# A decode-attention kernel: TensorE's unrolled matmuls put into loops, two weights loaded ahead of a third, and the output's heads split otherwise

## The chip, the cores and the metric

The kernel runs on one NeuronCore of a Trainium2 chip. Its engines are TensorE (PE: matmuls, with a weight load of its own, PEld), VectorE (DVE), ScalarE (ACT), GpSimd (POOL) and SyncE (SP, which issues DMAs); each runs its own program and they meet at semaphores. Sixteen DMA engines move data between HBM and the on-chip memory. The metric is the device time of one execution in microseconds; lower is better.

## The reference

One step of decoding for a batch of 2, one new token each, D = 512. Both halves start from `xn = layernorm(x)`.

```python
q = xn @ wq                       # 32 query heads of 128, from 512 x 4096 weights
scores = q . k * 128**-0.5        # 8 kv heads, 4 query heads share one; 32768 keys each
s = (softmax(scores) . v) @ wo    # 4096 x 512 weights

h  = gelu(layernorm(xn) @ w1); ... @ w2      # S = 1: every shifted part of it is padding
x1 = xn + 0
g  = silu(x1 + gelu(layernorm(x1) @ w3) @ w4)   # F = 1792
out = x + s * g
```

With one token the shifts of the w1/w2 branch push every row out, so its contribution is zero, and the kernel loads neither weight. The caches, 2 x 8 x 32768 x 128 in bf16 each for k and v, are nearly all of the data.

## The kernel before, in words

A *group* is one (batch, kv head) pair; there are 16. For each, 8 MB of K and 8 MB of V are loaded, each by one DMA from SyncE's queue (the last group's in halves). K has three slots of 4 MB in `kbuf`, V two in `vbuf`: K of group m+1 takes the one free slot and the one whose scores are finished first, V of group m+1 the place of V of group m.

**SyncE's queue** fixes the order of the loads: wq, w3, w4 and K of group 0 without a wait (L310 to L313), two small ones for x, V of group 0 once the w4 matmuls are done (L454; w3 and w4 lie in `vbuf`), four small ones for g (L457), then K and V of groups 1 to 15 by turns (L461 to L473), and last the output weights wo in six parts (L474 to L479). K of group m waits for TensorE's last use of the slot's old scores (`pe.sem`, raised at L703), V of group m for ScalarE's count of finished groups (`ac.sem`, L495).

**The prologue** (L333 to L459) makes xn, its second layernorm, constants out of an identity, and from 4 small transposes the columns `xT`. Then come 32 matmuls with wq (L403, four column strips of TensorE side by side) into `sc[0]` and `sc[1]`, two VectorE transposes (L408), q_sb, one spreading matmul (L413), and `qr` (L416). GpSimd makes from it, for every group, the weights `z` of the score matmuls (L505, L506). After that stand 16 matmuls with w3 (L424), the gelu on VectorE and ScalarE, 14 matmuls with w4 (L439), and silu, which gives g.

**A group.** VectorE transposes K in 16 pieces (L589) through four buffers `T`. TensorE makes the scores in two halves, `sc[0]` and `sc[1]`, of 8 x 4 matmuls each (L698). Between the halves stand 4 f32 matmuls that gather the *previous* group's output, `oT` (`head_oT`, L660), and in the second half, after its fifth piece, one that turns it, `xp` (`head_xp`, L666). VectorE takes the maxima (`peak`, L568), scales the previous group's output (`head_on`, L543 to L552), and picks its row (`head_out`, L559 to L565). A matmul of `S` (L710) spreads the maxima, ScalarE takes the exponential (L491), VectorE transposes it (L608), and TensorE multiplies with V (L722, 2 x 32 matmuls), with small filler matmuls ahead (`fill`, L673); a last matmul sums the exponentials (L729). TensorE counts the turn in a register and branches back (L733, L734).

**The output** (L737 to L774) gathers the last group, then applies wo. Heads 0 to 3 use one wide matmul (L740) that spreads their outputs, VectorE's `own_part` (L630, L634), and 16 matmuls into `qrb`. Head k = 4, below `KC` = 5, adds 4 matmuls of 512 columns there (L760). For heads 5 to 7, 4 x 4 matmuls of 128 columns each go straight into `pro` (L768). ScalarE copies `qrb` to `wsum` (L646), and 4 f32 matmuls with `comb` (L750, eight passes) add that to `pro`, ahead of head 6's. VectorE multiplies with g and adds x (L647, L648), and two DMAs store it.

`LateQueue` keeps the prologue's TensorE instructions and `place()` writes them out just ahead of the loop. `take(eng, s, n)` waits for a semaphore and lowers it by what it waited for. `t_tv` counts TensorE's steps for VectorE (`used`, `sum_of`, `out_of`, `turned` give the counts), `t_vt` VectorE's steps for TensorE.

Of the kernel before, what the change touches and what calls it, by code (L numbers as in the profile page):

```python
# [7 lines left out]
F32 = mybir.dt.float32  # L8
# [13 lines left out]
T_BUFS = 4  # L22
# [44 lines left out]
class LateQueue(Queue):  # L67
# [13 lines left out]

    def place(self):
        for emit, need, inc in self.kept:
            for s, v in need[:-1]:
# [34 lines left out]
def kernel(  # L119
# [37 lines left out]
    KC = 5  # L157
# [19 lines left out]
    Ts = [sb(f"T{i}", [128, W], I32) for i in range(T_BUFS)]  # L177
# [38 lines left out]
    qT = Ts[0].bitcast(F32)  # L216
# [13 lines left out]
    sc = [bank(f"sc{i}") for i in range(NPART)]  # L230
# [49 lines left out]
    t_vt, t_vg, t_tv = (sem(f"t_{n}") for n in ("vt", "vg", "tv"))  # L280
# [7 lines left out]
    wq3 = kbuf_wq[:, 0:DK * HD].rearrange("p (k f) -> p k f", k=DK)  # L288
    W4O = DK * Fdim
# [17 lines left out]
    with tc.tile_critical(sync_engine=mybir.EngineType.Pool, no_gpsimd_drain=True):  # L307
        nc.scalar.wait_ge(t_shift, n_out).then_inc(t_shift, -n_out)

        sp.op(lambda e: e.dma_start(out=kbuf_wq[:, 0:DK * HD], in_=A_wq.rearrange("(p k) f -> p (k f)", k=DK)), inc=(d_wq, 16))  # L310
# [17 lines left out]
        po.op(lambda e: e.memset(ob[:, :], 0.0), inc=(t_ob, 1))  # L328
# [5 lines left out]
        ve.op(lambda e: e.memset(S[:, 0:NPART * rep], 1.0), inc=(t_tv, 1))  # L334
        ve.op(lambda e: e.memset(pro[:, :], 0.0))
        ve.op(lambda e: e.memset(sc[0][:, :], 0.0))
        e_s00 = ve.op(lambda e: e.memset(sc[1][:, :], 0.0))
        e = ve.op(lambda e: e.tensor_copy(out=xf[:, :], in_=x_bf[:, :]), (d_x, 16))
# [51 lines left out]

        treg = qrb[:, :].bitcast(BF16)
        for k in range(DK):
# [4 lines left out]
            in_=treg[:, 0:64 * DK].rearrange("p (k s c) -> p s k c", k=DK, s=2)[:, :, :, 0:B]), e, (d_wq, 16))  # L397
        HH = Hq // NPART
        for i in range(NPART):
            for k in range(DK):  # L400
                for n in range(NQ):
                    last = k == DK - 1 and n == NQ - 1
                    e = pe.op(lambda t, i=i, k=k, n=n: t.matmul(  # L403
                        sc[i][32 * n:32 * n + B, :], lhsT=xT[:, k, :],
                        rhs=wq3[:, k, :].rearrange("p (h n y) -> p h n y", n=NQ, y=32)[:, i * HH:(i + 1) * HH, n, :],
                        start=(k == 0), stop=(k == DK - 1), tile_position=(0, 32 * n)),
                        e_xT, e_s00, inc=last)
            e = ve.op(lambda v, i=i: v.transpose(out=qT[:, i * 512:(i + 1) * 512], in_=sc[i][:, :]), e)  # L408
# [9 lines left out]


        FQ = Fdim // NQ  # L420
        for k in range(DK):
            for n in range(NQ):
                last = k == DK - 1 and n == NQ - 1
                e = pe.op(lambda t, k=k, n=n: t.matmul(  # L424
                    pro[32 * n:32 * n + B, 0:FQ], lhsT=xT[:, DK + k, :],
                    rhs=w3v[:, k, n * FQ:(n + 1) * FQ].rearrange("p (y f) -> p f y", y=32),
                    start=(k == 0), stop=(k == DK - 1), tile_position=(0, 32 * n)), (d_w3, 16), inc=last)
        e = ve.op(lambda v: v.transpose(out=h4[:, :], in_=pro[:, 0:FQ]), e)
        e_hf = ve.op(lambda v: v.tensor_copy(
            out=hf[:, :].rearrange("p (f b) -> p f b", b=B), in_=h4[:, :].rearrange("p (f c) -> p f c", c=32)[:, :, 0:B]), e)  # L430
        e = ve.op(lambda v: v.tensor_mul(out=x2[:, :], in0=hf[:, :], in1=hf[:, :]), e_hf)
        e = ve.op(lambda v: v.tensor_scalar(out=x2[:, :], in0=x2[:, :], scalar1=0.044715, scalar2=1.0, op0=ALU.mult, op1=ALU.add), e)
        e = ve.op(lambda v: v.tensor_mul(out=inner[:, :], in0=hf[:, :], in1=x2[:, :]), e)
        e = ac.op(lambda v: v.activation(out=th[:, :], in_=inner[:, :], func=ACT.Tanh, scale=GELU_C), e)
        e = ve.op(lambda v: v.tensor_scalar(out=th[:, :], in0=th[:, :], scalar1=0.5, scalar2=0.5, op0=ALU.mult, op1=ALU.add), e)
        e = ve.op(lambda v: v.tensor_mul(out=h_bf[:, :], in0=hf[:, :], in1=th[:, :]), e, (d_w4, 16))
        h2 = sc[1]
        for f in range(FK):
            e_h2 = pe.op(lambda t, f=f: t.matmul(  # L439
                h2[0:B, :], lhsT=h_bf[:, f * B:(f + 1) * B], rhs=w4v[:, f, :],  # L440
                start=(f == 0), stop=(f == FK - 1)), e, inc=f == FK - 1)
        e_tf = ve.op(lambda v: v.tensor_add(out=t_f[:, :], in0=xn[:, :], in1=h2[0:B, :]), e_h2)
        e = ac.op(lambda v: v.activation(out=sig[:, :], in_=t_f[:, :], func=ACT.Sigmoid), e_tf)
        e_g = ve.op(lambda v: v.tensor_mul(out=g[:, :], in0=t_f[:, :], in1=sig[:, :]), e)
# [16 lines left out]
        for m in range(1, NG):  # L461
            base = m % 2
            if m < NG - 1:
                sp.op(lambda e, m=m, base=base: e.dma_start(
                    out=kbuf[:, base * SLOT:(base + NPART) * SLOT], in_=row_view(A_k_cache, *groups[m])),
                    (pe.sem, pe_0 + m), e_q, inc=(t_k[0], 16))
            else:
                for i, h in enumerate(order(m)):
                    sp.op(lambda e, m=m, h=h, base=base: e.dma_start(
                        out=kbuf[:, (base + h) * SLOT:(base + h + 1) * SLOT],  # L470
                        in_=row_view(A_k_cache, *groups[m])[:, h * SLOT:(h + 1) * SLOT]),
                        (pe.sem, pe_0 + m), inc=(t_k[i], 16))
            load_v(m, (ac.sem, ac_0 + m))  # L473
# [6 lines left out]

        def take(eng, s, n=1):
            eng.wait_ge(s, n).then_inc(s, -n)  # L482

# [46 lines left out]
        def used(par, n):  # L530
            return t_tv, par * N_T + n + 2 + (n >= NR) + (n >= NR + 5)
# [4 lines left out]
        def out_of(par, last=False):  # L536
            return t_tv, par * N_T + (2 if last else NR + 2)

        def turned(par, last=False):
            return t_tv, par * N_T + (3 if last else NR + 8)  # L540

        def head_on(c, par=0, last=False, behind=None):
# [8 lines left out]
            nc.vector.wait_ge(*out_of(par, last))  # L551
            ins = nc.vector.tensor_mul(  # L552
                out=on[:, :, :], in0=oT[:, :].unsqueeze(1).broadcast_to([128, NQ, rep]), in1=recm[:, :, :]).wait_op(*e, "sem-ge")
            if last:
                ins.then_inc(t_vt, 1)
                behind()
# [69 lines left out]
        e_wd, e_ws, e_s = ((pe.sem, pe.n + NG + i) for i in (1, 2, 3))  # L626
# [12 lines left out]
        head_on(c, last=True, behind=own_part)  # L639
        e_oX[NG - 1] = head_out(c, last=True)  # L640
        for b in range(B):
            m, n = b * Hkv + KC, Hkv - KC - (b == B - 1)
            e_oXz = ve.op(lambda v, b=b, m=m, n=n: v.tensor_copy(
                out=oXz[:, 0:n, :, OJ * (1 + b) - 1], in_=oX[:, 1 + m:1 + m + n, :]), e_oX[m + n - 1], e_xz0)
# [36 lines left out]
        pe.n, pe.seen = prologue.n + NG, prologue.seen  # L681
# [7 lines left out]
        with nc.body("pe_groups", valid_engines=[PE]):  # L689
            for i in range(NPART):  # L690
                for r in range(NR):
                    if r % 2 == 0:
                        take(nc.tensor, t_vt, 2)
                    Tb = Ts[(i * NR + r) % T_BUFS][:, :].bitcast(BF16).rearrange("p (b c e) -> p b c e", b=NB, e=2)
                    zc = (NR - 1 - r) * rep
                    for nb in range(NB):
                        for w in range(2):
                            ins = nc.tensor.matmul(  # L698
                                sc[i][:, :], lhsT=z[:, nb, w, zc:zc + 128], rhs=Tb[:, nb, :, w],
                                start=(r == 0 and nb == 0 and w == 0),  # L700
                                stop=(r == NR - 1 and nb == NB - 1 and w == 1))
                            if i == 0 and r == NR - 1 and nb == 0 and w == 0:
# [31 lines left out]
            nc.br_lt(turn, NG, on_true="pe_groups", on_false="pe_output", engines=[PE])  # L734


        with nc.body("pe_output", valid_engines=[PE]):  # L737
            head_oT()
# [5 lines left out]
            take(nc.tensor, t_vt)  # L744
            head_xp()
            for i, (a, c, r0, r1) in enumerate(wo_parts):
                if i == 3:
# [5 lines left out]
                for k in range(a, c):  # L753
                    pe.wait(e_oXz if k >= KC else e_oX[(B - 1) * Hkv + k], (d_wo[i], n_wo[i]), *((e_wide,) if i == 0 else ()))
                    for r in range(r0, r1):
# [9 lines left out]
                        for n in range(NQ):  # L765
# [4 lines left out]
                                start=(i == 2 and r == r0 and n < OQ), stop=(last and n >= NQ - OQ), tile_position=(0, 32 * q)),  # L770
                                inc=(last and n == NQ - 1))
                    if i == 2:
                        warm(1)
# [38 lines left out]
```

## Time and profile before

| | |
|---|---|
| median of 3 runs (655.59 to 655.71) | 655.71 us |
| profiled execution, from its first to its last instruction | 654.1 us |
| mean granted TensorE clock | 0.880 |
| HBM read | 280.50 MB, 429 GB/s over the span |
| busy: PE, PEld | 417.4 us (64%), 159.3 us (24%) |
| busy: DVE, ACT, POOL | 379.4 us (58%), 39.7 us (6%), 10.3 us (2%) |

The profile shows one execution. A row of a group of instructions gives line, engine, operation, output and inputs, count, busy microseconds, and then the idle time of the engine just before them with what ended it. A row of the timeline begins with start and duration. The rows of the DMA view give the packets of a queue that start in a stretch, their MB, and the time that they take as a share of 16 engines; `q1` is the data queue, `q8` carries instructions.

### The profile page before, as it was taken

What the parts mean: (1) busy time and instruction counts of PE and PEld (TensorE: products, weight loads), DVE (VectorE), ACT (ScalarE), POOL (GpSimd) and SP (SyncE); (2) the same over time, 40 slices, a digit from 0 to 9 for tenths busy, and PEclk for the clock granted to TensorE, in tenths of its full rate; (3) what the DMA queues carried; (4) which work ended last, traced back from release to release, by engine and by line L of the source; (5) the groups of instructions that cost most, each with busy time, mean ns of one, the idle gap of its engine ahead of it and who ended that gap; (6) DMA issues with size and microseconds to landing.
All of it is one profiled execution on the core that took longest, in us unless ns stands there. A gap on an engine that the chain in (4) does not pass through costs nothing. (4 is left out here: it accounts for less than half of the span.)

```text
span 654.1 us, 6304 instructions
## 1 busy us (share of the span) xinstructions
PE 417.4 (64%) x2476; PEld 159.3 (24%) x2476; DVE 379.4 (58%) x541; ACT 39.7 (6%) x90; POOL 10.3 (2%) x44
## 2 busy tenths in 40 slices
PE   1437386574858747485774838667484865748876
PEld 0013132221313212131321313222131322213223
DVE  5348193673919457291854729276481936738772
ACT  1200101000010100001000010100001010000101
POOL 1000000000000000000000000000000000000000
PEclk9859889697997969899796989969698896979999
DMA  8999999999999999998999999999999899999997
GB/s 367 435 449 449 442 393 449 445 449 401 437 445 449 433 405 449 445 449 389 449 445 449 417 421 445 449 445 393 449 445 449 389 449 445 449 425 411 437 429 292
DMA packets 6246, 280.54 MB, mean 429 GB/s; under 512 B 730, under 2 KB 868, under 8 KB 1380
## 3 DMA queue, kind: packets, MB, share of 16 engines
q1 hardware_dynamic: 6232, 280.50, 99.2%
q8 instruction: 2, 0.03, 0.0%
q10 hardware_dynamic: 12, 0.00, 0.0%
HBM read 280.50 MB, written 0.00 MB: 429 GB/s over the span
## 5 line engine op out<-in xcount | busy, mean ns | idle before, releaser
L589 DVE STREAM_TRANSPOSE T<-kbuf 128x1024 int32<-128x1024 int32 x256 | 294.8, 1211 | 180.1 <-DMA kbuf<-in_A_k_cache_dram 173.2
L698 PE MATMUL sc<-T,z 128*128 128x512 bf16 x1024 | 273.1, 420 | 179.5 <-PEq L482 179.2
L698 PEld LDWEIGHTS sc<-T,z 128*128 128x128 bf16 x1024 | 98.9, 104 | 346.6 <-issue 260.2
L722 PE MATMUL o<-vbuf,pt 128*16 128x512 bf16 x1024 | 70.4, 379 | 17.7 <-PEq L482 17.7
L491 ACT ACTIVATE ep<-sc,shift 128x512 bf16<-128x512 f32 x32 | 21.7, 683 | 502.7 <-ACTq L482 502.7
L722 PEld LDWEIGHTS o<-vbuf,pt 128*16 128x16 bf16 x1024 | 27.3, 88 | 64.9 <-issue 42.8
L568 DVE TENSOR_REDUCE mx<-sc 128x1 f32<-128x512 f32 x32 | 21.5, 672 | 30.1 <-PE sc L698 30.1
L673 PE MATMUL pro<-ob,comb 128*2 128x512 f32 x66 | 33.7, 592 | 0.0
L608 DVE STREAM_TRANSPOSE pt<-ep 128x512 bf16<-128x512 bf16 x32 | 22.6, 708 | 15.0 <-ACT ep L491 15.0
L710 PE MATMUL S<-mxr,same_h 128*128 128x448 f32 x32 | 15.8, 576 | 18.4 <-PEq L482 18.4
L660 PEld LDWEIGHTS oT<-sel_o,ob 128*128 128x128 f32 x136 | 17.7, 191 | 3.4 <-issue 0.7
L729 PE MATMUL S<-sm,ones_f 128*128 128x448 f32 x32 | 16.3, 592 | 0.0
L660 PE MATMUL oT<-sel_o,ob 128*128 128x4 f32 x136 | 16.2, 242 | 0.0
L600 DVE TENSOR_REDUCE shift<-S 128x1 f32<-128x64 f32 x16 | 3.6, 225 | 18.8 <-PE S L710 18.8
L496 ACT COPY ob<-o 128x512 f32<-128x512 f32 x16 | 9.4, 587 | 78.6 <-ACTq L482 78.6
L513 POOL COPY oX<-oXs 128x4 bf16 (+1 forms) x16 | 3.0, 188 | 518.7 <-POOLq L482 518.7
L710 PEld LDWEIGHTS S<-mxr,same_h 128*128 128x128 f32 x32 | 4.8, 188 | 26.1 <-issue 26.1
L572 DVE TENSOR_SCALAR mxr<-row_of,mx 128x32 f32<-128x32 f32 x32 | 7.7, 241 | 1.1
L673 PEld LDWEIGHTS pro<-ob,comb 128*2 128x2 f32 x66 | 4.2, 83 | 14.0 <-issue 10.4
L393 PE MATMUL qrb<-ident,xs_bf 34*128 34x34 bf16 x4 | 0.3, 198 | 11.1 <-DVE xs_bf L356 11.1
L729 PEld LDWEIGHTS S<-sm,ones_f 128*128 128x128 f32 x32 | 4.8, 188 | 6.9 <-issue 6.9
L506 POOL TENSOR_TENSOR z<-qr,quad 128x64 bf16<-128x64 bf16 x16 | 4.7, 294 | 103.2 <-POOLq L482 87.7
(100 smaller groups left out, 78.5 us busy)
## 6 DMA issues: line engine op xcount, KB each, us to landing
kbuf<-in_A_k_cache_dram SPq DMA_DIRECT2D x2, 4096.0 KB, 22.4
vbuf<-in_A_v_cache_dram SPq DMA_DIRECT2D x2, 4096.0 KB, 21.7
kbuf<-in_A_wq_dram SPq DMA_DIRECT2D x1, 4096.0 KB, 12.4
vbuf<-in_B_w_dram SPq DMA_DIRECT2D x2, 1792.0 KB, 18.0
kbuf<-in_A_wo_dram SPq DMA_DIRECT2D x1, 2048.0 KB, 30.8
kbuf<-in_A_wo_dram SPq DMA_DIRECT2D x3, 512.0 KB, 31.9
kbuf<-in_A_wo_dram SPq DMA_DIRECT2D x1, 384.0 KB
kbuf<-in_A_k_cache_dram SPq DMA_DIRECT2D x15, 27.5
```

What stands on the lines that cost most here:

```text
L491: nc.scalar.activation(out=ep[i][:, :], in_=sc[i][:, :], func=ACT.Exp, scale=inv_sqrt_dh, bias=shift[:, :], accum_out=rs[:, i:i + 1]).then ...
L496: nc.scalar.copy(out=ob[:, :], in_=o[:, :]).then_inc(t_ob, 1)
L568: ins = nc.vector.tensor_reduce(out=mx[:, i:i + 1], in_=sc[i][:, :], axis=AX.X, op=ALU.max)
L572: ins = nc.vector.tensor_scalar_mul(out=mxr[:, i, :], in0=row_of[:, :], scalar1=mx[:, i:i + 1]).wait_op(*c.at(t_d), "sem-ge")
L589: ins = nc.vector.transpose(out=Ts[n % T_BUFS][:, :].rearrange("p (b t k) -> p t b k", b=NB, t=RT), in_=kt[:, r * W:(r + 1) * W].rearrange ...
L608: ins = nc.vector.transpose(out=pt[h][:, :, :].rearrange("p r (t h) -> p t r h", h=rep), in_=ep[order(par).index(h)][:, :].rearrange("p (t ...
L660: ins = nc.tensor.matmul(oT[:, :], lhsT=ob[:, t * Dh:(t + 1) * Dh], rhs=sel_o[:, t, :], start=(t == 0), stop=(t == VT - 1))
L673: nc.tensor.matmul(pro[0:B, :], lhsT=comb[:, 0:B], rhs=ob[:, :], start=True, stop=True)
L698: ins = nc.tensor.matmul(sc[i][:, :], lhsT=z[:, nb, w, zc:zc + 128], rhs=Tb[:, nb, :, w], start=(r == 0 and nb == 0 and w == 0), stop=(r = ...
L710: nc.tensor.matmul(S[:, NPART * rep:NPART * (rep + SREP * 32)].rearrange("p (s c) -> p s c", s=SREP), lhsT=same_h[:, :], rhs=mxr[:, :, :]. ...
L722: ins = nc.tensor.matmul(o[32 * j:32 * j + VT * rep, :], lhsT=pt[h][:, r, a * VT * rep:(a + 1) * VT * rep], rhs=vt[:, u * VT:(u + 1) * VT, ...
L729: nc.tensor.matmul(S[:, 0:SSUM * NPART * rep].rearrange("p (s c) -> p s c", s=SSUM), lhsT=ones_f[:, :], rhs=sm[:, :, :].rearrange("p i h - ...
```

## The change

TensorE's program goes from 634 instructions to 449.

- **q.** The 32 strip matmuls become a loop of 8 turns (`q_part`) of 4 matmuls with 512 columns; ScalarE copies each result of 2 rows into `q_row` (`q_out`, also a loop) while TensorE uses the other half of `sc2`; 4 VectorE transposes follow. `q_row` lies in the `T` buffers, cleared by a new GpSimd memset.
- **w4.** 12 of its 14 matmuls become a loop of 6 turns.
- **Order.** w3 and w4 load ahead of wq, and their stage stands ahead of q's.
- **Scores.** The two halves become a loop of 2 turns. `xp` moves behind it, `oT` to the end of the turn, and TensorE waits for the next two transposes *before* the branch back. A branch hint stands at the head of every turn. `pe.sem` is raised once in each half now.
- **VectorE** does the second `peak` ahead of `head_out`.
- **Output.** `xp` of the last group goes ahead of the wide matmul. `KC` is 7, so heads 4 to 6 go through `qrb` and head 7 alone straight into `pro`; the `comb` matmuls come before the sixth part of wo (the first row of head 7); the filler `warm(1)` is gone.

```diff
+    def loop(self, nc, n, emit, *events, inc=True):
+        self.kept.append(((nc, n, emit), self._new(events), inc))
...
     def place(self):
         for emit, need, inc in self.kept:
+            if isinstance(emit, tuple):
+                nc, n, body = emit
...
+                with nc.Fori(0, n, engines=[PE]) as i:
+                    body(self.eng, i).then_inc(*((self.sem, 1) if inc is True else inc))
+                continue
...
-    KC = 5
+    KC = 7
...
-        sp.op(lambda e: e.dma_start(out=kbuf_wq[:, 0:DK * HD], in_=A_wq.rearrange("(p k) f -> p (k f)", k=DK)), inc=(d_wq, 16))
         sp.op(lambda e: e.dma_start(out=vbuf[:, 0:W4O], in_=B_w3.rearrange("(p k) f -> p (k f)", k=DK)), inc=(d_w3, 16))
         sp.op(lambda e: e.dma_start(out=vbuf[:, W4O:W4O + FK * D], in_=B_w4.rearrange("(p f) d -> p (f d)", f=FK)), inc=(d_w4, 16))
+        sp.op(lambda e: e.dma_start(out=kbuf_wq[:, 0:DK * HD], in_=A_wq.rearrange("(p k) f -> p (k f)", k=DK)), inc=(d_wq, 16))
...
+        def w4_part(t, j):
+            for i in range(W4N):
+                ins = t.matmul(
+                    h2[0:B, :], lhsT=h_bf[:, bass.ds(j * W4N * B + (1 + i) * B, B)],
+                    rhs=vbuf[:, bass.ds(j * W4N * D + W4O + (1 + i) * D, D)], start=False, stop=False)
+            return ins
...
+        pe.loop(nc, (FK - 2) // W4N, w4_part)
...
+        def q_part(t, c):
+            take(t, t_q)
+            out_c = sc2[0:B, bass.ds((c & 1) * 512, 512)]
             for k in range(DK):
...
+                ins = t.matmul(
+                    out_c, lhsT=xT[:, k, :], rhs=wq3[:, k, bass.ds(c * 512, 512)],
+                    start=(k == 0), stop=(k == DK - 1))
+            return ins
+
+        pe.loop(nc, NC, q_part, e_tf, (d_wq, 16), inc=(t_qp, 1))
...
+        with nc.Fori(0, NC - 1, engines=[ACTE]) as c:
+            dst, src = q_out(c)
+            nc.scalar.copy(out=dst, in_=src).then_inc(t_q, 1)
...
+        for n in range(NQ):
+            e = ve.op(lambda v, n=n: v.transpose(
+                out=qT[32 * n:32 * n + 32, :], in_=q_row.rearrange("p (h n y) -> p n h y", n=NQ, y=32)[:, n, :, :]), e, e_row0)
...
+                peak(c, 1, *used(par, NT - 1))
                 head_out(c, par)
-                peak(c, 1, *used(par, NT - 1))
...
-            for i in range(NPART):
+            hint_p = nc.tensor.mark_branch_hint_location()
+            with nc.Fori(0, NPART, engines=[PE]) as i:
                 for r in range(NR):
...
-                                sc[i][:, :], lhsT=z[:, nb, w, zc:zc + 128], rhs=Tb[:, nb, :, w],
+                                sc2[:, bass.ds(i * 512, 512)], lhsT=z[:, nb, w, zc:zc + 128], rhs=Tb[:, nb, :, w],
...
-                    if i == 1 and r == 4:
-                        head_xp()
-                if i == 0:
-                    head_oT()
+            take(nc.tensor, t_on)
+            head_xp()
...
             nc.regs_alu(turn, turn, 1, op=ALU.add)
-            nc.br_lt(turn, NG, on_true="pe_groups", on_false="pe_output", engines=[PE])
+            head_oT()
+            nc.tensor.wait_ge(t_vt, 2)
+            nc.tensor.br_lt(turn, NG, on_true="pe_groups", on_false="pe_output").branch_hint(hint_p)
...
         with nc.body("pe_output", valid_engines=[PE]):
-            head_oT()
+            take(nc.tensor, t_vt, 2)
+            head_xp()
             pe.wait(e_sp, e_oX[NG - 2])
...
-            take(nc.tensor, t_vt)
-            head_xp()
             for i, (a, c, r0, r1) in enumerate(wo_parts):
-                if i == 3:
+                if i == 5:
```

More of the change, by code (lines that the diff above doesn't have):

```diff
@@ L176 @@
     vbuf = sb("vbuf", [128, 2 * SLOT], BF16)
-    Ts = [sb(f"T{i}", [128, W], I32) for i in range(T_BUFS)]
+    T_all = sb("T", [128, T_BUFS * W], I32)
+    Ts = [T_all[:, i * W:(i + 1) * W] for i in range(T_BUFS)]
     ep = [sb(f"ep{i}", [128, RT * 32], BF16) for i in range(NPART)]
@@ L228 @@
     oXz = sb("oXz", [128, Hkv - KC, NQ, OJ - 1 + OM], BF16)
-    sc = [bank(f"sc{i}") for i in range(NPART)]
+    sc2 = bank("sc", 512 * NPART)
+    sc = [sc2[:, 512 * i:512 * (i + 1)] for i in range(NPART)]
     o = bank("o")
@@ L333 @@
         ve.op(lambda e: e.memset(o[:, :], 0.0))
-        ve.op(lambda e: e.memset(S[:, 0:NPART * rep], 1.0), inc=(t_tv, 1))
-        ve.op(lambda e: e.memset(pro[:, :], 0.0))
+        for t in (S[:, 0:NPART * rep], oT[:, :]):
+            ve.op(lambda e, t=t: e.memset(t, 1.0), inc=(t_tv, 1))
+        e_pro0 = ve.op(lambda e: e.memset(pro[:, :], 0.0))
         ve.op(lambda e: e.memset(sc[0][:, :], 0.0))
         e_s00 = ve.op(lambda e: e.memset(sc[1][:, :], 0.0))
+        nc.vector.sem_inc(t_q, NPART)
         e = ve.op(lambda e: e.tensor_copy(out=xf[:, :], in_=x_bf[:, :]), (d_x, 16))
@@ L388, with take @@
         hint_v = nc.vector.mark_branch_hint_location()
+        def take(eng, s, n=1):
+            eng.wait_ge(s, n).then_inc(s, -n)
         treg = qrb[:, :].bitcast(BF16)
@@ L396 @@
             out=xT[:, :, :].rearrange("p (s k) b -> p s k b", s=2),
-            in_=treg[:, 0:64 * DK].rearrange("p (k s c) -> p s k c", k=DK, s=2)[:, :, :, 0:B]), e, (d_wq, 16))
-        HH = Hq // NPART
-        for i in range(NPART):
-            for k in range(DK):
[L401 to L408, printed above, removed]
+            in_=treg[:, 0:64 * DK].rearrange("p (k s c) -> p s k c", k=DK, s=2)[:, :, :, 0:B]), e)
@@ new lines @@
+        FQ = Fdim // NQ
+        for k in range(DK):
+            for n in range(NQ):
+                last = k == DK - 1 and n == NQ - 1
+                e = pe.op(lambda t, k=k, n=n: t.matmul(
+                    pro[32 * n:32 * n + B, 0:FQ], lhsT=xT[:, DK + k, :],
+                    rhs=w3v[:, k, n * FQ:(n + 1) * FQ].rearrange("p (y f) -> p f y", y=32),
+                    start=(k == 0), stop=(k == DK - 1), tile_position=(0, 32 * n)), e_xT, (d_w3, 16), e_pro0, inc=last)
+        e = ve.op(lambda v: v.transpose(out=h4[:, :], in_=pro[:, 0:FQ]), e, e_row0)
@@ new lines @@
+        e_hf = ve.op(lambda v: v.tensor_copy(
+            out=hf[:, :].rearrange("p (f b) -> p f b", b=B), in_=h4[:, :].rearrange("p (f c) -> p f c", c=32)[:, :, 0:B]), e)
+        e = ve.op(lambda v: v.tensor_mul(out=x2[:, :], in0=hf[:, :], in1=hf[:, :]), e_hf)
+        e = ve.op(lambda v: v.tensor_scalar(out=x2[:, :], in0=x2[:, :], scalar1=0.044715, scalar2=1.0, op0=ALU.mult, op1=ALU.add), e)
+        e = ve.op(lambda v: v.tensor_mul(out=inner[:, :], in0=hf[:, :], in1=x2[:, :]), e)
+        e = ac.op(lambda v: v.activation(out=th[:, :], in_=inner[:, :], func=ACT.Tanh, scale=GELU_C), e)
@@ new lines @@
+        e = ve.op(lambda v: v.tensor_scalar(out=th[:, :], in0=th[:, :], scalar1=0.5, scalar2=0.5, op0=ALU.mult, op1=ALU.add), e)
+        e = ve.op(lambda v: v.tensor_mul(out=h_bf[:, :], in0=hf[:, :], in1=th[:, :]), e, (d_w4, 16))
+        h2 = sc[1]
+        W4N = 2
+        def w4_part(t, j):
[4 more added lines that the diff above has]
+            return ins
@@ new lines @@
+        assert (FK - 2) % W4N == 0
+        pe.op(lambda t: t.matmul(h2[0:B, :], lhsT=h_bf[:, 0:B], rhs=w4v[:, 0, :], start=True, stop=False), e, inc=False)
+        pe.loop(nc, (FK - 2) // W4N, w4_part)
+        e_h2 = pe.op(lambda t: t.matmul(h2[0:B, :], lhsT=h_bf[:, (FK - 1) * B:FK * B], rhs=w4v[:, FK - 1, :], start=False, stop=True))
+        e_tf = ve.op(lambda v: v.tensor_add(out=t_f[:, :], in0=xn[:, :], in1=h2[0:B, :]), e_h2)
+        e = ac.op(lambda v: v.activation(out=sig[:, :], in_=t_f[:, :], func=ACT.Sigmoid), e_tf)
@@ new lines, in q_out @@
+        def q_out(c):
+            take(nc.scalar, t_qp)
+            return q_row[0:B, bass.ds(c * 512, 512)], sc2[0:B, bass.ds((c & 1) * 512, 512)]
+        ac.wait(e_row0)
+        with nc.Fori(0, NC - 1, engines=[ACTE]) as c:
+            dst, src = q_out(c)
+            nc.scalar.copy(out=dst, in_=src).then_inc(t_q, 1)
+        dst, src = q_out(NC - 1)
+        e = ac.op(lambda v: v.copy(out=dst, in_=src))
+        for n in range(NQ):
+            e = ve.op(lambda v, n=n: v.transpose(
+                out=qT[32 * n:32 * n + 32, :], in_=q_row.rearrange("p (h n y) -> p n h y", n=NQ, y=32)[:, n, :, :]), e, e_row0)
@@ L417 @@
             out=qr[:, :, :, :, :].rearrange("p n e b h -> p (n e b h)"), in_=qrb[:, 0:NB * 2 * B * Hq]), e)
[L420 to L444, printed above, removed]
         def load_v(m, *events):
@@ L638 @@
         e_wide = (ve.sem, ve.n + 2)
-        head_on(c, last=True, behind=own_part)
+        head_on(c, behind=own_part)
         e_oX[NG - 1] = head_out(c, last=True)
```

56 lines of the change are left out of this document (32 added, 24 removed).

## The prediction

> **What bounds the kernel now.** I read the page's totals first, then SyncE's own waits, then the chain of work that ended last, and then the DMA view in narrow stretches.
>
> ```profile
> span 654.1 us, 6304 instructions
> ...
> q1 hardware_dynamic: 6232, 280.50, 99.2%
> q8 instruction: 2, 0.03, 0.0%
> ...
> kbuf<-in_A_k_cache_dram SPq DMA_DIRECT2D x15, 27.5
> ```
>
> The packets of the data queue fill 99.2% of 16 engines' span. The kernel is one stream of 280.5 MB, and the compute engines only have to free buffers early enough.
>
> ```profile
> SPq L448 <- ACTq L495: 275.9, 14, 19.7
> ```
>
> Before each V load SyncE waits 19.7 us for its buffer (275.9 over 14), and a load lands 27.5 us after its issue, so some 8 us of work is always queued and the stream has no gap. An edit of compute costs nothing until it delays an issue by most of that. So two things can set the time: how long each DMA engine needs for its share, and what follows the last landing.
>
> ```profile
> 617.12 33.53 DMA kbuf<-in_A_wo_dram
> ...
> 650.69 0.64 PE pro L768 x16
> ...
> 651.35 0.29 DVE sg L647
> ...
> 651.67 0.28 DVE out L648
> ```
>
> The chain at the end is the last wo part, 16 small matmuls, two VectorE operations and the store. The last part lands at 650.64 although the stream is nearly dry earlier, which the DMA view shows in stretches (packets that start in each, MB, share of 16 engines). The rows are, in order, 66.6 to 67.4 us; 71.7 to 71.8; 72.6 to 72.8; 649.5 to 649.6; 649.6 to 650.7.
>
> ```profile
> q1 hardware_dynamic: 16, 1.05, 302.2%
> ...
> q8 instruction: 1, 0.02, 57.6%
> ...
> q1 hardware_dynamic: 1, 0.07, 91.4%
> ...
> q8 instruction: 1, 0.02, 60.0%
> ...
> q1 hardware_dynamic: 18, 0.03, 6.6%
> ```
>
> Before 71 us the 16 engines start their packets together, 16 within 0.8 us. At 71.7 one engine carries instructions instead: 57.6% of 16 engines for 0.1 us is 0.92 us. Its next data packet starts by itself at 72.6 to 72.8, and nothing later gives it the 0.92 us back, because every engine is full. At the end the last 18 packets trickle out over 1.1 us at 6.6% of the engines' time, which is one engine in 16 (6.25%). I read this as the same engine: **one instruction fetch in the first turn costs about 0.9 us at the end.** The second fetch, at 649.5, falls into idle time of the other engines.
>
> **The change part by part.** TensorE alone has a program long enough to matter here (634 instructions; VectorE's is about 160).
>
> *The first-turn fetch.* TensorE's loop over groups runs 16 times, and only its first turn, with the last part of the program, brought a fetch. After the change the loop is still there, shorter, and so is the part behind it. Whether its first turn still fetches is the main unknown: gain between 0 and 0.92 us. I take 0, because the second fetch, as large as the first, came when by my count of the program under 100 of its instructions were left; a fetch that merely runs ahead comes whether the program goes on or not. [...]
>
> *The tail.* These are the rows of the timeline on which it rests.
>
> ```profile
> 645.20 0.22 PE L740 MATMUL sc<-T,sel_w 128*128 128x128 bf16 x1
> ...
> 645.45 0.17 DVE L552 TENSOR_TENSOR on<-oT,recm 128x16 bf16<-128x16 f32 x1 [0.52 <-PE oT L660]
> 645.54 0.28 DVE L630 TENSOR_TENSOR T<-sc,mask 128x128 f32<-128x128 f32 x1
> 645.86 0.38 DVE L634 TENSOR_REDUCE T<-T 128x32 bf16<-128x128 f32 x1
> ...
> 646.41 1.04 PE L760 MATMUL qrb<-kbuf,T 128*2 128x512 bf16 x16
> ...
> 647.29 0.39 PE L760 MATMUL qrb<-kbuf,oX 128*2 128x512 bf16 x4
> ...
> 647.74 0.59 ACT L646 COPY T<-qrb 128x512 f32<-128x512 f32 x1 [3.57 <-PE qrb L760]
> ...
> 649.07 0.81 PE L750 MATMUL pro<-T,comb 128*4 128x128 f32 x8
> ```
>
> TensorE now waits for `on` before it leaves the loop, and the xp matmul goes ahead of the wide one. So the wide matmul, at 645.20 before, comes after `on` (645.62), the branch and xp: about 646.2. VectorE's 0.28 and 0.38 follow, and the 16 matmuls start near 647.2, 0.8 later. That is hidden: they end at 648.2, heads 4 and 5 take 0.39 each, and TensorE is free by 649.1. With KC = 7 heads 5 and 6 take 4 matmuls each instead of 16, the copy of `qrb` waits for head 6, and the 8 half-speed passes of `comb` go behind head 7's first 12 matmuls. The part of head 6 is used at 649.74 (the start of the second group of 16 in the row below), so the copy runs from about 650.19 to 650.78.
>
> ```profile
> 649.74 0.61 PE L768 MATMUL pro<-kbuf,oXz 128*4 128x128 bf16 x16
> ```
>
> Sixteen such matmuls take 0.61 with 0.22 for one, so one starts every 0.026. The 12 issue from 650.69 to 651.00. The 8 passes take 0.54 to issue (0.81 less 0.27 for one), to 651.55, and the last 4 end 0.30 later, at 651.86. Before they ended at 651.33, or 651.31 without the rounding of the chain. **Cost 0.55 us**; bounds 0.25 (the passes meet a wait that was there anyway) and 0.9 (0.81 whole).
>
> *The start.* w3 and w4 go first, then wq, then K of group 0: the same bytes, and no gap between, so nothing for the stream. But q is now computed last, in a loop of 8 turns handed to ScalarE, which copies two rows at a time, and VectorE does 4 transposes. VectorE's first transpose of group 0 waits for z, which waits for q.
>
> ```profile
> 2.40 0.62 POOL L326 MEMSET z<- 128x624 bf16 x1
> ...
> 13.29 0.17 DVE L395 COPY xT<-qrb 128x16 bf16<-128x16 bf16 x1 [0.18 <-DMA kbuf<-in_A_wq_dram]
> ...
> 17.59 0.58 DVE L409 TENSOR_TENSOR q_sb<-T,cls 128x256 bf16<-128x256 f32 x1
> ...
> 18.43 3.42 PE L424 MATMUL pro<-vbuf,xT 128*2 128x448 bf16 x16
> ...
> 19.05 0.29 POOL L506 TENSOR_TENSOR z<-qr,quad 128x64 bf16<-128x64 bf16 x1 [15.42 <-DVE qr L416]
> ...
> 21.90 0.65 DVE L428 STREAM_TRANSPOSE T<-pro 128x448 f32<-128x448 f32 x1 [2.93 <-PE pro L424]
> ...
> 24.23 3.18 PE L439 MATMUL sc<-vbuf,h_bf 128*2 128x512 bf16 x14 [2.38 <-DVE h_bf L436]
> ...
> 27.45 0.67 DVE L442 TENSOR_TENSOR shared<-shared,sc 2x512 f32<-2x512 f32 x1 [3.27 <-PE sc L439]
> ...
> 41.14 5.75 DVE L589 STREAM_TRANSPOSE T<-kbuf 128x1024 int32<-128x1024 int32 x5 [10.51 <-DMA kbuf<-in_A_k_cache_dram]
> ...
> 619.10 1.97 PE L698 MATMUL sc<-T,z 128*128 128x512 bf16 x8 [0.28 <-PEq L482]
> ```
>
> From xT (13.5): w3's matmuls 3.4, to 16.9; the small operations from 21.90 to 24.23 again, 2.4, to 19.3; w4's 14 matmuls 3.2 and about 1 for six turns, to 23.5; the sum 0.7, to 24.2. A turn of q's loop has 4 matmuls of 0.227 (3.18 over 14), 0.91, and its register steps, waits and branch, which no row shows: between 0 and 1.1 (four times the 0.28 that TensorE loses at a wait in the last row). ScalarE's copy, near the 0.59 of its copy of `qrb`, lies beside. I take 1.4 a turn: 11.2, and 0.7 for the last copy, to 36.1. Four transposes at 1.15 (5.75 over 5) make 40.7, and from q_sb to z it is 1.75 (17.59 to 19.34), so group 0 starts near 43 instead of 41.14. Bounds: 41.1, where K's landing decides, and 52, with a turn of 2.5 at half clock.
>
> ```profile
> 0.90 0.40 SPq L310 DMA_DIRECT2D kbuf<-in_A_wq_dram  x1
> ...
> 52.20 0.35 SPq L464 DMA_DIRECT2D kbuf<-in_A_k_cache_dram  x1
> ...
> 72.27 0.33 SPq L448 DMA_DIRECT2D vbuf<-in_A_v_cache_dram  x1
> ```
>
> The next row is of the DMA view from 1.8 to 2.0 us, where the first packets start.
>
> ```profile
> q1 hardware_dynamic: 4, 0.13, 257.9%
> ```
>
> That delay is covered: V of group 1 is issued at 72.27, and K of group 1, issued at 52.20, lands 27.5 later, at 79.7; with 1.0 from an issue to its first packet (0.90 to 1.9) the cover is 6.4 us. So group 0 may start as late as 47.5. **Cost 0.** GpSimd's new memset of 4096 columns is done long before VectorE needs it at 16.9: by 0.62 for 624 columns it takes 4.1 from about 3.2.
>
> ```profile
> 52.69 0.95 PE L660 MATMUL oT<-sel_o,ob 128*128 128x4 f32 x8
> ...
> 65.61 0.23 DVE L600 TENSOR_REDUCE shift<-S 128x1 f32<-128x64 f32 x1 [1.17 <-PE S L710]
> ```
>
> *The loop.* The oT matmuls move from between the score halves to the turn's end, where TensorE waits for K anyhow; they free 0.95 us of each turn. A branch per half, a hint, and a wait for two transposes ahead of the branch add some 0.5. Behind that wait stand only the next scores. xp waits for `on`, made long before; head_out moves behind the second peak, into VectorE's idle 1.17 before the shift. All of it lies inside the 8 us of queued loads: cost 0, and it would take over 5 us a turn to cost anything.
>
> **Sum.** 654.1 + 0.55 = 654.65 of span. The median of 655.71 stands 1.6 above the span, which I keep: 656.26, say 656.3.
>
> **The rivals.**
> *The change removes the fetch.* For it: one fetch in 16 turns looks like code that was not yet there, and there is less code. Against it: the second fetch with nothing left to bring. All 16 engines then end by 649.6; the last part is usable some 0.33 after its last packet, as now (packets to 650.7, last 4 matmuls from 651.03, which is 651.33 less 0.30), at 649.9, and TensorE's own tail decides: heads 4 to 6 done by 649.25, the copy by 649.85, 12 matmuls beside it, the passes to 650.5, the last 4 by 650.8. That is 0.5 better: 655.2.
> The next row is of the stretch view (busy time of the engines, then the granted clock, here 0.61).
>
> ```profile
> 20.00:24.00 4.00, 1.85 (x12) 0.13 (x4) 1.57 (x7) 0.53 (x2) 0.00 (x0) 0.61 1.39 600
> ```
>
> *Group 0 starts late (slower).* If a turn of q's loop costs over 2 us, group 0 starts past 47.5 and V of group 1 is issued after K has landed; the stream idles by the excess, for good. At 2.5 us a turn the start is 52 and the price 4.5: 657 to 661. For it: the clock was down to 0.61 from 20 to 24 us, with TensorE busy half of it; against it: q's loop keeps TensorE busier than that.
>
> *A fetch in every turn.* A hint that is armed 16 times could fetch 16 times; on one engine that is 16 x 0.92 = 14.7 us, up to 670. VectorE runs a hint before its loop, at about 13 us, and no instruction packet is seen until 71.7, so this is unlikely.
>
> **How the numbers follow.** Fetch stays 0.46 (656.3), fetch gone 0.33 (655.2), group 0 late 0.13, a fetch each turn 0.03, an unforeseen gain below 654.4 0.05. A measurement of this kernel can tell about 0.2%, 1.3 us, from no change: 654.4 to 657.0 is within. The first two cases lie inside: same 0.79, slower 0.16, faster 0.05. The range of 654.8 to 657.6 holds both, their bounds of 0.3 either way, and the mild end of the late start; it leaves out some 0.2.
>
> **What would show it.** The instruction queue: one packet near 70 to 86 us and a lone trickle of one engine at the end (forecast), none and all engines ending together (first rival), many (third). In the chain, the comb passes between the last landing and the last 4 matmuls. VectorE's first transpose of group 0 at 43, and SyncE's issue of V of group 1 ahead of 78.7. I am wrong if the DMA queue shows a gap before the tail, or if the last landing moves by more than 1 us.

## The result, and the profile after

The changed kernel takes 658.21 us (median of 5 runs, 658.10 to 658.61); the kernel before took 655.71 on the same chip. The ratio is 1.0037, with a 95% interval of 1.0024 to 1.0050. The change makes it slower, and the time lies 0.6 us above the range of 654.8 to 657.6. What happened is the rival that had 0.13: group 0 starts late and the stream loses time for good, though not for the reason that the rival gave.

The page's totals of the changed kernel show a span 2.3 us longer, the same bytes, a smaller share of the DMA engines, and, on queue 8, one instruction packet in place of two.

```profile
span 656.4 us, 6559 instructions
...
q1 hardware_dynamic: 6232, 280.50, 98.9%
q8 instruction: 1, 0.02, 0.0%
```

Its timeline on GpSimd and VectorE (start, duration, operation) shows how the lateness begins and where it has got to.

```profile
3.10 3.50 POOL L345 MEMSET T<- 32x4096 f32 x1
4.29 2.59 DVE L358 CAST shared<-x_bf 2x512 f32<-2x512 bf16 x1 [1.01 <-DMA x_bf<-in_A_x_dram]
...
13.94 0.16 DVE L418 COPY xT<-qrb 128x16 bf16<-128x16 bf16 x1
...
38.11 5.04 DVE L481 STREAM_TRANSPOSE kbuf<-T 32x1024 f32<-32x1024 f32 x4 [10.61 <-ACT T L479]
43.19 0.58 DVE L483 TENSOR_TENSOR q_sb<-kbuf,cls 128x256 bf16<-128x256 f32 x1
...
44.87 0.48 DVE L505 MEMSET qrb<- 128x512 f32 x1 [0.18 <-DVE qr L490]
45.41 0.48 DVE L506 MEMSET pro<- 128x512 f32 x1
45.80 2.34 DVE L632 STREAM_TRANSPOSE T<-kbuf 128x1024 int32<-128x1024 int32 x2
```

The cast of x, 2 rows of 512, takes 2.59 us while GpSimd's new memset of q_row runs beside it, and ends just behind that memset's end at 6.60. Group 0 starts at 45.80; it was 41.14. SyncE's issues move with it, and beside them stand, from the DMA view of 46 to 90 us, the times from issue to landing of K and V of group 1.

```profile
57.06 0.36 SPq L511 DMA_DIRECT2D kbuf<-in_A_k_cache_dram  x1
77.09 0.33 SPq L495 DMA_DIRECT2D vbuf<-in_A_v_cache_dram  x1
```

```profile
kbuf<-in_A_k_cache_dram SPq DMA_DIRECT2D x1, 23.3
vbuf<-in_A_v_cache_dram SPq DMA_DIRECT2D x1, 24.6
```

K(1) lands at 57.06 + 23.3 = 80.4 and V(1) at 101.7, 21.3 later. The same two rows of the kernel before:

```profile
kbuf<-in_A_k_cache_dram SPq DMA_DIRECT2D x1, 28.7
vbuf<-in_A_v_cache_dram SPq DMA_DIRECT2D x1, 27.9
```

There K(1) lands at 52.20 + 28.7 = 80.9 and V(1) at 100.2, 19.3 later. So nothing is lost up to K(1), and 2.0 us between it and V(1). V(1) was issued 3.3 us ahead of K(1)'s landing, and that was too late: in the trace only 12 to 15 of the 16 DMA engines carry a packet from 79.0 to 81.3 us, where the kernel before has all 16 at work. The packets that start from 78 to 84 us, before and then after, show the same (a packet is counted with its whole time, so a share can pass 100%).

```profile
q1 hardware_dynamic: 63, 3.08, 118.5%
```

```profile
q1 hardware_dynamic: 47, 2.03, 88.3%
```

The chain's end shows what follows the last landing.

```profile
619.22 33.02 DMA kbuf<-in_A_wo_dram
652.25 0.14 issue
652.38 0.50 PE pro L813 x12
652.88 0.44 PE pro L795 x8
653.32 0.13 PE pro L813 x4
653.45 0.02 issue
```

The last part lands at 652.25 (650.64), and from there to the last matmul's end it is 1.20 us in place of 0.69: the comb passes stand between the 12 and the 4 matmuls, as forecast.

### The profile page after: what moved, and what is told of

Read it like the earlier page. It is cut to its first block, busy times and chain, and to the rows that moved or that the text cites. A ratio compares the mean times of both kernels' runs of the same rounds, so it can differ in the third digit from the quotient of the medians.

```text
span 656.4 us, 6559 instructions
## 1 busy us (share of the span) xinstructions
PE 427.7 (65%) x2411; PEld 160.5 (24%) x2443; DVE 386.9 (59%) x543; ACT 44.3 (7%) x98; POOL 14.0 (2%) x45
## 5 line engine op out<-in xcount | busy, mean ns | idle before, releaser
L705 PEld LDWEIGHTS oT<-sel_o,ob 128*128 128x128 f32 x128 | 15.5, 191 | 11.1 <-issue 11.1
L481 DVE STREAM_TRANSPOSE kbuf<-T 32x1024 f32<-32x1024 f32 x4 | 4.9, 1235 | 10.7 <-ACT T L479 10.6
L463 PE MATMUL sc<-kbuf,xT 128*2 x32 | 8.2, 377 | 3.8 <-issue 2.3
```

What stands on the lines that cost most here:

```text
L463: ins = t.matmul(out_c, lhsT=xT[:, k, :], rhs=wq3[:, k, bass.ds(c * 512, 512)], start=(k == 0), stop=(k == DK - 1))
L705: ins = nc.tensor.matmul(oT[:, :], lhsT=ob[:, t * Dh:(t + 1) * Dh], rhs=sel_o[:, t, :], start=(t == 0), stop=(t == VT - 1))
```

## The experiments

**Theory:** the late start costs the time. **Rivals:** the tail, the order of the first loads, the loops with their branches, and instruction fetches. The table gathers what the traces of all kernels show. Lands and starts are in us of the span; "lead" is K(1)'s landing less V(1)'s issue; "behind" is from the last landing to the last matmul's end. An empty field means that the last landing was not on the chain that ended last. Each ratio is to runs of the kernel before on the same chip; it took 656.14 us beside e1 to e4, 656.02 beside e5 to e8, 655.96 beside e9 and e10, and 655.92 beside e11.

| kernel | group 0 starts | V(1) issued | lead | V(1) less K(1) landing | last landing | behind | median us | ratio to before (95%) |
|---|---|---|---|---|---|---|---|---|
| before | 41.14 | 72.27 | 8.6 | 19.3 | 650.64 | 0.69 | 655.71 | 1 |
| after | 45.80 | 77.09 | 3.3 | 21.3 | 652.25 | 1.20 | 658.21 | 1.0037 (1.0024 to 1.0050) |
| e1 | 41.68 | 73.60 | 6.6 | 19.4 | 650.19 | 2.54 | 658.50 | 1.0046 (1.0031 to 1.0060) |
| e2 | 45.97 | 77.27 | 3.2 | 21.8 | | | 660.56 | 1.0064 (1.0051 to 1.0077) |
| e3 | 46.96 | 78.38 | 3.7 | 19.4 | 652.14 | 0.69 | 657.96 | 1.0030 (1.0019 to 1.0040) |
| e4 | 43.74 | 74.89 | 5.9 | 19.3 | 650.61 | 0.68 | 655.92 | 0.9997 (0.9988 to 1.0006) |
| e5 | 43.59 | 74.54 | 6.1 | 19.3 | 650.45 | 1.20 | 656.24 | 1.0002 (0.9993 to 1.0012) |
| e6 | 42.45 | 74.33 | 6.0 | 19.3 | 650.24 | 1.20 | 656.02 | 0.9999 (0.9990 to 1.0008) |
| e7 | 42.68 | 74.56 | 6.3 | 19.4 | 650.67 | 1.21 | 656.56 | 1.0011 (1.0002 to 1.0020) |
| e8 | 41.14 | 72.41 | 7.3 | 19.3 | | | 662.16 | 1.0093 (1.0078 to 1.0108) |
| e9 | 50.77 | 82.61 | 6.7 | 19.3 | 659.58 | 1.20 | 665.88 | 1.0156 (1.0142 to 1.0170) |
| e10 | 41.79 | 73.06 | 7.8 | 19.3 | 650.62 | 0.68 | 655.98 | 1.0002 (0.9993 to 1.0011) |
| e11 | 41.04 | 72.78 | 8.0 | 19.3 | 650.59 | 0.67 | 656.00 | 1.0000 (0.9991 to 1.0009) |

**e1 and e2: one part of the change undone.** e1 is the changed kernel with q by 32 strip matmuls and two transposes, as in the kernel before, and so without the memset of q_row; e2 is the changed kernel with the tail of before.

```diff
-        pe.loop(nc, NC, q_part, e_tf, (d_wq, 16), inc=(t_qp, 1))
...
+                    e = pe.op(lambda t, i=i, k=k, n=n: t.matmul(
+                        sc[i][32 * n:32 * n + B, :], lhsT=xT[:, k, :],
```

> The changed kernel with q made as before: 32 strip matmuls and two transposes in place of the loop of 8 turns, the ScalarE copies, the memset and the 4 transposes; everything else as changed. Theory 'late start' (group 0 starts 4.7 us late, V of group 1 is issued too late, and the stream stalls for good): group 0 starts again when K has landed, near 41 us, and 1.9 to 2.1 us come back: 656.1 to 656.4. Rival 'loops' (the branches, the register steps and the hint of the score loop cost something in every turn): 658.0 to 658.3, unchanged. Rival 'order' (w3 and w4 ahead of wq slow the start of the stream): unchanged too.

```diff
-    KC = 7
+    KC = 5
...
-                if i == 5:
+                if i == 3:
```

> The changed kernel with the output of before: KC 5, the comb matmuls ahead of head 6, the rest as changed. Theory 'tail' (the comb passes behind the last landing cost 0.5 us): 657.7, and the chain behind the last landing is 16 matmuls of 0.64 us again. Rival (the tail is hidden or is part of the stall): 658.1 to 658.3. [...]

e1 starts early, loses nothing between K(1) and V(1), and has its last landing 2.06 us ahead of the changed kernel's, as the theory wants. Yet it gains no time, and neither run has a time that was expected. (e1's six runs spread from 657.59 to 661.19, and its trace is of the shortest.) The ends of the chains, of e1 and then of e2, say why.

```profile
650.33 0.28 PE pro L794 x4
650.61 1.16 issue
651.77 0.39 PE pro L794 x8
```

```profile
652.13 0.38 PE pro L813 x11
652.51 2.19 issue
654.70 0.79 PE pro L813 x21
```

Among matmuls whose data are there, TensorE stands still for 1.16 and 2.19 us. Both programs are longer than the changed one (499 and 503 instructions, counted in the way that gives 455 for it), and both keep its hint. One instruction packet of 0.92 us goes with each wait: it starts at 649.5 in e1 and at 652.3 in e2, and TensorE goes on 1.4 and 1.5 us behind its end. This is e2's, from the DMA view of 652.2 to 652.4 us.

```profile
q8 instruction: 1, 0.02, 28.8%
```

So e2's gain in the tail was eaten by a wait for code, and a new question arose: what does the hint do to the code's arrival? e7, e8 and e10 take it up.

**e3 and e4: the late start alone.** The kernel before, with nine or four memsets of 0.48 us chained on VectorE ahead of group 0, once K(0) has landed.

```diff
+        nc.vector.wait_ge(t_k[0], 16)
+        for _ in range(9):
+            e_s0 = ve.op(lambda v: v.memset(pro[:, :], 0.0), e_s0)
```

> The kernel before, with VectorE busy for 4.8 us (9 memsets of a bank, one behind the other) after K of group 0 has landed and ahead of its first transpose: only group 0 is late, to about 46 us as in the changed kernel. Theory 'late start': V of group 1 is issued near 77 and the stream stalls: 657.4 to 657.9. The prediction's own rule (cover until 47.5) and the rivals 'loops' and 'order': 655.7, no change.

> As the run with 9 memsets, with 4: VectorE busy for 2.1 us, group 0 at about 43.3, V of group 1 issued near 74.5, 5 us ahead of the landing. Theory 'late start' with a cover of about 3 us in the stream: 655.7 to 655.9, no change. If a delay cost in proportion from the first microsecond: 656.6.

These are SyncE's two issues and the landings in e3.

```profile
58.30 0.35 SPq L467 DMA_DIRECT2D kbuf<-in_A_k_cache_dram  x1
78.38 0.33 SPq L448 DMA_DIRECT2D vbuf<-in_A_v_cache_dram  x1
```

```profile
kbuf<-in_A_k_cache_dram SPq DMA_DIRECT2D x1, 23.8
vbuf<-in_A_v_cache_dram SPq DMA_DIRECT2D x1, 23.1
```

K(1) itself lands at 82.1, 1.2 late, and the end moves by 1.5 (657.96 us, where 657.4 to 657.9 was expected): a start of 46.96, still ahead of the 47.5 from which the prediction let it cost, is not free. The load that came too late is another one than in the changed kernel. In e3 V(0), issued at 30.31, lands 30.0 later, at 60.3, only 2.0 us behind K(1)'s issue, and from 59.8 to 61.0 us only 6 to 15 of the engines carry a packet. In the changed kernel K(1) was issued 4.0 us ahead of V(0)'s landing (61.1), and nothing was lost there. A start of 43.74 is free: e4 has the time of before. So, with the 45.80 of the changed kernel, the bound lies between 43.74 and 45.80.

**e5 and e6: the late start mended in the changed kernel.** e5 moves the memset of q_row behind h_bf; e6 also makes q's transposes in two halves, the first behind the fourth of the eight copies.

```diff
-        e_row0 = po.op(lambda e: e.memset(q_row, 0.0))
...
+        e_row0 = po.op(lambda e_: e_.memset(q_row, 0.0), e)
```

> The changed kernel, with GpSimd's 3.5-us memset of q_row moved behind h_bf (from 3.1 us to about 20 us). If the memset is what made VectorE's cast of x take 2.59 instead of 0.41 us: the cast is back near 0.4 us, xT is written at about 13.2 (13.94), group 0 starts at about 44.9 (45.80), V(1) is issued at about 76.2 (77.09), and the time is 657.0 to 657.8. If the cast is slow for another reason: it stays at 2.5 us or so, group 0 at 45.8, the time at 658.2.

> As e5, and q's four transposes in two halves, the first behind the fourth of q's eight copies. If the late start of group 0 is what the change costs: group 0 starts at 42.3 to 43.5, V(1) is issued at 73.6 to 74.8, no engine idles between 60 and 90 us by more than 0.3 us, the last packet lands 1.5 to 2 us earlier than in the changed kernel, and the time is 655.9 to 656.6. If the cost were the order of the first loads (w3 and w4 ahead of wq) or the loops, the time stays above 657.5 though group 0 is early.

The timeline of e5:

```profile
4.34 0.41 DVE L357 CAST shared<-x_bf 2x512 f32<-2x512 bf16 x1 [1.06 <-DMA x_bf<-in_A_x_dram]
...
11.81 0.16 DVE L417 COPY xT<-qrb 128x16 bf16<-128x16 bf16 x1
...
17.92 3.50 POOL L437 MEMSET T<- 32x4096 f32 x1 [14.29 <-DVE h_bf L436]
```

The memset takes its 3.50 us as in the changed kernel, in a place where VectorE waits for TensorE, and the cast is back at 0.41. xT is there 2.13 us earlier, group 0 starts 2.21 earlier, and the whole loss is gone: 656.24. I had expected group 0 only 0.9 earlier, and 657.0 to 657.8, too little a gain, because I had compared xT with the kernel before, where it waits for wq (13.29) and the cast is covered. The bytes moved between 60 and 640 us, from the DMA view of the changed kernel and then of e6, show the loss in the stream by itself: 0.44 MB, which at 251.22 MB in 580 us is 1.0 us for the mean of the engines; the latest of them lost more.

```profile
q1 hardware_dynamic: 4584, 250.78, 99.9%
```

```profile
q1 hardware_dynamic: 4618, 251.22, 100.0%
```

e6 came out as expected, at the time of the kernel before: with an early start, neither the loops nor the order of the first loads cost anything that can be told. That its group 0 starts 1.1 us ahead of e5's moves V(1) by only 0.2 and the time by nothing that can be told.

**e7 and e8: the hint.** e7 is e6 without the hint of the loop over groups; e8 is the kernel before with nothing but that hint.

```diff
-            hint_p = nc.tensor.mark_branch_hint_location()
...
-            nc.tensor.br_lt(turn, NG, on_true="pe_groups", on_false="pe_output").branch_hint(hint_p)
+            nc.tensor.br_lt(turn, NG, on_true="pe_groups", on_false="pe_output")
```

> As e6, with the branch hint of TensorE's loop over the groups left out. If the hint is what took the instruction fetch out of the stream (without it, the block behind the loop's is fetched in the first turn): a queue-8 packet of 16 KB and 0.9 us stands between 60 and 80 us, one engine ends about 0.9 us behind the others, and the time is 0.5 to 1.0 us above e6. If the fetch went because the program is short: no such packet, and the time of e6 within 0.3 us.

> The kernel before with nothing but the branch hint on TensorE's loop over the groups (638 instructions). If the hint decides: the fetch at 71.8 us is gone and no engine is 0.92 us behind at the end, but TensorE waits 1 to 2.2 us in the output part for its code, and the time is 656.2 to 657.5. If the hint does nothing: the fetch stays at about 72 us and the time at 655.7 within 0.2 us.

In e7, though its program is as short as the changed kernel's, one fetch stands in the DMA view between 74 and 75 us, of 5.8% x 16 = 0.93 us on one engine:

```profile
q8 instruction: 1, 0.02, 5.8%
```

Its last landing is 0.43 us behind e6's. So the fetch went because of the hint, not because the program is short. All thirteen traces agree: the six kernels without the hint (before, e3, e4, e7, e10, e11) have one instruction packet between 71 and 79 us, the seven with it have none there.

In e8 the chain of waits has this row in the output part, behind the first of its oT matmuls and before the last seven:

```profile
643.47 5.65 issue
```

The fetch is gone from the first turn there too, but TensorE waits 5.65 us behind the loop, and the time is 662.16. I had the sign and not the size (656.2 to 657.5 expected). These are the packets that start from 646 to 648 us.

```profile
q1 hardware_dynamic: 226, 0.81, 99.6%
q8 instruction: 1, 0.02, 2.9%
```

The instruction packet starts at 646.8, 3.3 us into the wait, while data packets still fill the engines, and TensorE goes on 1.4 us behind its end, as in e1 and e2. That it stood behind data packets would account for the longer wait; no run tests it.

**e10: short tail, no hint.** e7 with the tail of before (as e2's edit).

> As e7 (early start, no hint), with KC 5 and the sums' columns a part earlier, as in the kernel before: 502 TensorE instructions by the count that gives 455 for the changed kernel. If the wait of 2.19 us in e2's output part came from the hint (the block behind the loop's is not fetched in the first turn): no wait for code in the output part, behind the last landing 0.64 us in place of 1.07, a queue-8 packet near 74 us, and the time 0.4 us under e7: 655.9 to 656.4. If it came from the length alone: the wait of 1 to 2 us stays and the time is 657 to 658.5.

At 502 instructions, one fewer than e2, there is no wait for code behind the last landing:

```profile
650.62 0.04 issue
650.66 0.64 PE pro L819 x16
651.30 0.02 issue
```

The time is 655.98, as expected. e2 differs from e10 in its late start too, but e8, with the hint as its one edit, says the same: in these kernels the hint takes an early fetch of 0.93 us on one engine away and puts a wait at the end of a program that is too long. The 455 instructions of the changed kernel are few enough, 499 are not; what lies between is not measured.

**e9 and e11: the first loads.** In e6 thirteen of the engines start a packet from 28.0 to 28.6 us and the other three at 29.3, some 1 us behind. e9 loads a quarter of wq's partitions ahead of w3; e11 is the kernel before with wq in two loads of half the columns.

```diff
+        sp.op(lambda e: e.dma_start(out=kbuf_wq[0:32, 0:DK * HD], in_=A_wq.rearrange("(p k) f -> p (k f)", k=DK)[0:32, :]), inc=(d_wq, 16))
```

> As e6, with the first 32 of wq's 128 partitions (32 packets of 32 KB) loaded ahead of w3, the other 96 behind w4. In e6 the first packets are w3's 14 KB ones, of 0.5 to 2.4 us, and at 28 us the 16 engines are spread from 28.0 to 29.3 us for the same bytes; in the kernel before, with 32-KB packets first, from 28.0 to 28.7. If the small first packets spread the engines, and the latest engine carries it to the end: spread at 28 us back to 0.7 us, last landing near 649.6 (650.24 in e6), time 655.2 to 655.6. If the spread comes from elsewhere (x's small packets among the first): last landing at 650.2, time 656.0 within 0.2 us.

```diff
+        for c in range(2):
+            cols = slice(c * DK * HD // 2, (c + 1) * DK * HD // 2)
```

> The kernel before with wq, its first load, in two loads of half the columns each (packets of 16 KB in place of 32 KB); order and everything else as before. If small packets at the very start spread the engines (e6: 28.0 to 29.3 us where they have moved the same bytes, before: 28.0 to 28.7), and the latest engine carries that to the end: spread to 29 us or more, the engines other than the one that fetched code end at 650.1 or later (649.5 before), and the time is 656.2 to 656.8. If it is w3's place ahead of wq, or something else of the changed kernel: spread and time as before, 655.9 within 0.2 us.

e9 missed by 10 us and says nothing of its question: its packets of the other 96 partitions, from 20 to 27 us, took 16 x 7 x 1.02 / 48 = 2.38 us each,

```profile
q1 hardware_dynamic: 48, 1.57, 102.0%
```

where the kernel before, from 5 to 10 us, has 16 x 5 x 1.016 / 67 = 1.21 for the same 32 KB:

```profile
q1 hardware_dynamic: 67, 2.20, 101.6%
```

e11 has the time of before, and its engines are not spread (28.2 to 28.6 us). That packets of 16 KB at the start cost time has fallen; what spreads the engines when w3 goes first stays open.

## Why the prediction failed, step by step

- **The stream bounds the kernel: right.** Every kernel here that lost time neither in the stream nor at TensorE's code came within 0.2% of the one before.
- **The cover of 6.4 us: wrong, and the step that failed first.** It let V(1) be issued up to 1.0 us ahead of K(1)'s landing, from the time that one issue takes to its first packet in an empty queue. The runs show leads of 3.2 and 3.3 us (e2, after) costing 2.5 and 2.0, and leads of 5.9 and more costing nothing. For the load ahead, K(1) over V(0), a lead of 2.0 cost 1.2 (e3) and one of 4.0 nothing (after). A landing is that of the last of 16 engines; the others run dry before it, as the 12 to 15 engines at work around 80 us show. So the start may not be later than some point between 43.74 and 45.80, where the prediction had 47.5. Of its own signs, V(1)'s issue ahead of 78.7 came (77.09) and did not protect the stream; the last landing moved by 1.61, over the 1 us that it had named as proof against itself.
- **GpSimd's memset at no cost: wrong, and the step that made group 0 late.** "Done long before VectorE needs it" asked who reads its result, and not who runs beside it. It took 2.18 us from VectorE's cast and 2.21 from group 0 (e5). In the trace the cast starts 1.19 us behind the memset and ends 0.28 us behind its end; by what means a memset on GpSimd holds VectorE up, no run shows.
- **The rest of the start: right in sum.** 43 was the estimate, 43.59 is e5's. The turn of q's loop is 1.36 (1.4), and four transposes 5.04 (4.6). These rows of the changed kernel's timeline are two turns; w4's matmuls, from 20.12 to 25.42, took 5.3 (4.2), and the early xT of e5 (11.81, where 13.29 was taken) made up for it. One term was overlooked: from q_sb to group 0 it is 2.61 us (1.75), because VectorE's two memsets of 0.48, of `qrb` and `pro`, stand there; the kernel before runs them from 29.61 on, long before group 0. Without the memset of q_row this cost no time (e5).

```profile
35.00 1.02 PE L463 MATMUL sc<-kbuf,xT 128*2 x4 [0.34 <-issue]
36.36 1.02 PE L463 MATMUL sc<-kbuf,xT 128*2 x4 [0.34 <-issue]
```

- **The rival's reason: wrong.** It wanted a turn of over 2 us at a low clock. The place and the sign were right, the cause was another.
- **The tail, +0.55: right.** 1.20 less 0.69 is 0.51.
- **The loop over groups at no cost: right.** In e5 and e6, which have the new loop, K(1) and V(1) land 19.3 us apart as before, and the last landing, at 650.45 and 650.24, is no later than the 650.64 before. The 0.5 a turn for branches, hint and wait was my estimate; no row shows it by itself.
- **The first-turn fetch stays: wrong.** It went, and the price of 0.92 for it was too high: e7 against e6 gives 0.43 at the last landing and 0.5 in the time (e7's runs spread from 656.13 to 658.26, e6's from 655.80 to 656.26). The forecast's reading, a fetch that merely runs ahead and comes whether the program goes on or not, fits e7, where a program as short as the changed one still fetches; the first rival's reason, less code, does not. Only the third rival asked what the hint does, and it looked for a fetch in every turn; the changed kernel has no instruction packet in any turn. e7 and e10, without a hint, each have a fetch of 0.93 us in the first turn, between 74 and 75 us, and no wait for code behind the last landing.
- **The sum.** From before to after the last landing moved by 1.61 and the part behind it by 0.51, together 2.12 of the span's 2.3. e5's last landing is 1.80 ahead of the changed kernel's, and that is the late start; the hint's gain of 0.43 goes the other way. The 0.2 or so that this leaves over is less than runs of one kernel differ here (the kernel before took 655.74 to 656.53 beside e5). With the start mended, the forecast's 0.6 above the kernel before does not come either: the tail's 0.51 and the hint's 0.43 all but cancel, and e6 has the 656.02 of the kernel before.

No version here beats the kernel before by what can be measured. e6 and e10 equal it: one has the fetch gone and the long tail, the other the fetch and the short tail.

## What to carry to other kernels

In a kernel that is one stream of loads, measure the cover as the lead of an issue over the landing ahead of it, and don't count on the time to a first packet: here that was 1.0 us, a lead of 3.3 cost 2.0, and leads of 4.0 and more cost nothing. Price a "free" memset on an idle engine by what runs beside it, not only by who reads it: here VectorE's cast beside it took 2.59 us in place of 0.41. A shorter program and a branch hint are one edit: here the hint kept the code's fetch out of the loop, and only the programs of 455 instructions got that without a wait at the end.

## What the runs showed of the hardware

- While a GpSimd memset of 32 x 4096 f32 ran (3.50 us), VectorE's cast of 2 x 512 took 2.59 us in place of 0.41 (after, e5).
- A branch hint on a loop of 16 turns removed the one fetch of 0.93 us in its first turn and put a wait of 1.16 us (499 instructions), 2.19 (503) or 5.65 (638) behind the loop; without the hint, programs of 454 and 502 had none behind the last landing (e7, e10). TensorE went on 1.4 to 1.5 us behind the end of the instruction packet.
- In e9, where wq's other 96 of 128 partitions are a load of their own, a 32-KB packet of it took 2.38 us; with all 128 in one load it took 1.21 (before). No run here varies the partitions alone, so the cause is not shown.
